# A fifth feature block in a seven-product (Strassen) matmul, and output stores by two column blocks

## The chip, the cores and the metric

The kernel runs on one core of one Trainium2 chip. The time is that of the device, in microseconds, for one execution of the whole program; less is better. TensorE (PE) does the matmuls, VectorE (DVE), ScalarE (ACT) and GpSimd (POOL) the elementwise work, and SyncE (SP) issues most DMAs; ACT issues some.

## What is computed

Decayed linear attention over 4 batches, 8 heads, 768 positions and 64 dimensions in blocks of 64, then a two-layer network with a leaky ReLU on 3072 tokens of 512 features (2048 hidden). All inputs are float32.

```python
for b in range(nb):                       # blocks of 64 positions
    intra = einsum('bhic,bhjc->bhij', qb, kb) * Dmask
    intra = einsum('bhij,bhjd->bhid', intra, vb)
    inter = einsum('bhid,bhde->bhie', qb * lam_pow, kv_state)
    out[:, :, sl] = intra + inter
    kv_state = lam_block * kv_state + einsum('bhsd,bhse->bhde', kb * rev_pow, vb)
x = out.transpose(0, 2, 1, 3).reshape(B * S, H * D)      # 3072 x 512
h = x @ w_in                                             # 3072 x 2048
return maximum(0.01 * h, h) @ w_out                      # 3072 x 512
```

## The kernel before

**Staging.** The 3072 tokens are 24 chunks of 128, or six groups of `T` = 512; two groups make a pair (`pr` = 0, 1, 2). The 2048 hidden features are eight blocks `p` of 256. A float32 operand is split into three parts, high, low and a middle one (`h`, `l`, `m`), and each product is three matmuls, one for each part.

First the attention of each chunk is done ("r"), and between the chunks the products with `w_in` ("up", group g, block p): 24 matmuls of 512 columns each. ACT applies the leaky ReLU and writes the tile `gs`, which goes to DRAM. For feature blocks below `NS` (4; `NS0` = 2 for the first pair) `sums` first makes six combinations on DVE, stored in `BB`; the others are stored plainly in `G`. The weights `w_out` are made ready meanwhile ("wo", "wp") and, for blocks below `NS`, `w_sums` ("ws") makes their combinations.

Then, from about 324 us, come the products with `w_out`, pair by pair. For a block under `NS`, the 2x2 block product (two groups against two halves of the features and of the outputs) is done with seven products, s(t, u), t = 1 to 7, instead of eight: unit u holds two feature blocks and 12 matmuls. Partial sums lie in the PSUM bank pairs X, Z, Y and V, with copies by ACT (`copy_banks`) and additions by ACT and DVE (`add_banks`) between the products. The other blocks are plain units n(p, group) of 24 matmuls. The last block's unit ("l") also transposes each of the four output column blocks on DVE (`turn_out`, L943) and stores them (`store_out`, L951); the very last group does this in `ending`.

**The ring.** Each unit loads its moving operand (L825, on SP), and ACT makes the high part (L828), DVE the low (L831) and the middle one (L835). There are five slots, so a unit's load is issued when the unit five places earlier has left PE. For product 4 a second block is loaded and subtracted first (L842, L843). PE's matmuls are at L723 (up) and L851 (units).

**Order.** `Plan` is a list scheduler: each operation is added with an engine, an assumed duration, the keys that it reads and writes, and a rank, mostly its place in the written list `seq`. `emit` takes whatever can start earliest by these durations, ties by rank, and so fixes the order on each engine ahead of time. A DMA is assumed to need 3.5 us more until it lands; a store on ACT counts 0.5 us and 0.1. Engines run their own order, so a wait holds up all that is queued behind it. `LEAD` lowers the rank of the preparation of units; `HOLD`, `WPR` and `WSR` shift the rank of steps in the last group's phase.

Of the kernel before, what the change touches and what calls it, by code (L numbers as in the profile page):

```python
# [166 lines left out]
def kernel(  # L167
# [35 lines left out]
    NS, NS0 = 4, 2  # L203
    WS0, WS1 = 1, 2
    LEAD = 8.0
    TURN_B = 2
    HOLD, WPR, WSR, LEAD0 = 0.15, 2.0, 0.0, 12.0
# [34 lines left out]
    gst = sb([P, 2, 2, T], "gs")  # L242
    gs = [gst[:, i] for i in range(2)]
# [3 lines left out]
    BB = [[dram.tile([P, 6 * 2 * T], F32, name=f"b{r}_{u}", tag=f"b{r}_{u}") for u in range((NS if r else NS0) // 2)] for r in range(NG // 2)]  # L247
# [405 lines left out]
    staging = [w32f, lowt.bitcast(F32), gs[1].rearrange("p f t -> p (f t)")]  # L653
    SK = [["w320", "w321"], ["low0", "low1"], ["gs1"]]
# [3 lines left out]
    def free_attention(x="att"):  # L658
        extra[x] = sb([P, NA if x == "att" else NB], x, F32R)

# [3 lines left out]
    def operand(z, p, t):  # L664

        if t >= 0:
            return W[p][z][:, t * NQ:(t + 1) * NQ]
        return more(z, p)[:, (-1 - t) * NQ:-t * NQ]
# [14 lines left out]

    def w_sums(p):

        j, jr, main, rest = (SK[0], SK[1], staging[0], staging[1]) if p >= NS0 else (["raw1", "zr"], ["raw2"], raw[1], raw[2])
        b = [main[:, i * NQ:(i + 1) * NQ] for i in range(4)] + [rest[:, i * NQ:(i + 1) * NQ] for i in range(3)]
        add("DMA", 1.5, lambda: nc.sync.dma_start(out=main, in_=WO[p]), [f"WO{p}0", f"WO{p}1"], j, rank=-3.0)

        def sub(o, x, y, op, reads, k_):  # L690
            add("DVE", 0.42, lambda: nc.vector.tensor_tensor(b[o], b[x], b[y], op=op), reads, k_)

        sub(5, 0, 1, ALU.subtract, j, jr)
        sub(1, 1, 3, ALU.add, [], j)
        sub(4, 1, 0, ALU.subtract, j, jr)
        sub(6, 2, 4, ALU.subtract, j, jr)
        for key, us, x, src, k_ in ((f"w{{}}{p}", 0.42, lambda z: W[p][z][:, NQ:2 * NQ], b[1], j),
                                   (f"e{{}}{p}", 0.95, lambda z: more(z, p), rest[:, :3 * NQ], jr)):
            h, l, m = [key.format(z) for z in "hlm"]
            add("ACT", 0.9 * us, lambda x=x, src=src: nc.scalar.activation(out=x(0), in_=src, func=AF.Copy, bias=0.0, scale=NEAR / S), k_, [h])  # L700
            add("DVE", us, lambda x=x, src=src: nc.vector.scalar_tensor_tensor(x(1), x(0).bitcast(F32), -S, src, op0=ALU.mult, op1=ALU.add),
                k_ + [h], [l])
            if p == NS - 1 and k_ is jr:
                add("ACT", 0.0, free_lows, [], jr + [m])
            minus(us, x, key)
# [71 lines left out]
    def sums(g, p, y, kg):  # L777
# [7 lines left out]
        d = BB[g // 2][p // 2].rearrange("p (k c g t) -> p k c g t", k=6, c=2, g=2)[:, :, p % 2, g % 2, :]  # L785
# [23 lines left out]
    def unit(src, keys, f=1, less=None):  # L809

        nonlocal n_ring
        j = slots[n_ring] if n_ring < len(slots) else RING[(n_ring - len(slots)) % NR]
        first, n_ring = j not in slots[:n_ring], n_ring + 1

        def wr(z):
            return [f"r{z}{j}"] + ([f"x{z}{j // 2}{cc}" for cc in range(GC)] if first and j < 4 else [])

        def m_slot():
            return ring[j][2].bitcast(F32)

        def g():
            return m_slot() if less is None else w32f

        def go():
            nc.sync.dma_start(out=m_slot().rearrange("p (f t) -> p f t", f=f), in_=src)  # L825

        def head():
            nc.scalar.activation(out=ring[j][0], in_=g(), func=AF.Copy, bias=0.0, scale=NEAR)  # L828

        def low():  # L830
            nc.vector.scalar_tensor_tensor(ring[j][1], g(), 1.0, ring[j][0].bitcast(F32), op0=ALU.mult, op1=ALU.subtract)  # L831

        def middle():
            h, l, m = ring[j]
            nc.vector.scalar_tensor_tensor(m, l.bitcast(F32), -S, h.bitcast(F32), op0=ALU.mult, op1=ALU.add)  # L835

        kg = [f"rm{j}"]
        add("DMA", 1.5, go, keys, wr("m"))
        if less is not None:
            x, k = less  # L840
            kg = ["w320", "w321"]
            add("DMA", 1.5, lambda: nc.sync.dma_start(out=w32f, in_=x), k, kg)  # L842
            add("DVE", 1.25, lambda: nc.vector.tensor_tensor(w32f, w32f, m_slot(), op=ALU.subtract), [f"rm{j}"], kg)  # L843
        add("ACT", 1.05, head, kg, wr("h"))
        add("DVE", 1.25, low, kg + [f"rh{j}"], wr("l"))
        add("DVE", 1.25, middle, [f"rh{j}", f"rl{j}"], [f"rm{j}"])
        return j
# [6 lines left out]
    def strassen(pr, t, u, lead):  # L854

        g = 2 * pr
        ps_ = (2 * u, 2 * u + 1)
# [3 lines left out]
        def block(kind):  # L861
            k = KINDS_B.index(kind)
            return BB[pr][u][:, k * 2 * T:(k + 1) * 2 * T], [f"{'B' if k < 4 else 'T'}{x}{p}" for x in (g, g + 1) for p in ps_]

        x, keys = block("6" if t == 4 else str(t))
        j = unit(x.rearrange("p (f t) -> p f t", f=1), keys, less=block("2") if t == 4 else None)
# [15 lines left out]
        add("PE", 0.227 * (13 if begins else 12), go, [f"r{z}{j}" for z in "hlm"] + [f"{'w' if w >= 0 else 'e'}{z}{p}" for z in "hlm" for p in ps_],  # L882
            ACC[d] + (ACC["Z"] if begins else []))

    def plain(pr, p, gi, lead, last=False, banks=None):
# [25 lines left out]
        for c in banks:  # L911
            some(c)
            turn_out(gi, c)
        for m in range(2):
            store_out(pr, gi, m, range(4), "AAAA")

    def ending(pr, gi, first, lead):
# [8 lines left out]
        for m in range(2):  # L926
            store_out(pr, gi, m, a, "SASA")
        for c in z:
            one(c)
        for m in range(2):  # L930
            for c in z:
                two(c, m * HT, HT)
                turn_out(gi, c, m * HT, HT)
            store_out(pr, gi, m, z, "SASA")

    otile = gst.rearrange("p x f (b c j) -> p (x f b) c j", c=4, j=C4)

    def turn_out(gi, c, lo=0, n=T):
        nonlocal n_o
        n_o += 1  # L940
        d, i = BANKS[gi][c]
        b, o = acc[d][i], otile[:, lo // C4:(lo + n) // C4, c, :]
        add("DVE", 0.1 + 0.6 * n / T, lambda: nc.vector.transpose(out=o, in_=b[:, lo:lo + n].rearrange("p (b i) -> p b i", i=C4)), [ACC[d][i]],  # L943
            [f"o{c}{m}" for m in range(lo // HT, (lo + n) // HT)] + (["gs0", "gs1"] if n_o <= 4 else []), rank=-1.5)

    def store_out(pr, gi, m, cs, queues):
        t0, n, w = (2 * pr + m) * T + gi * HT, HT // C4, len(cs) * C4

        def store(a, q):
            c0 = a * P + cs[0] * C4  # L950
            q.dma_start(out=out[t0:t0 + HT, c0:c0 + w].rearrange("(b i) j -> i b j", i=C4),  # L951
                        in_=otile[a * C4:(a + 1) * C4, m * n:(m + 1) * n, cs[0]:cs[-1] + 1, :].rearrange("i b c j -> i b (c j)"))

        for a, x in enumerate(queues):
            e, q = {"S": ("DMA", nc.sync), "A": ("ACT", nc.scalar)}[x]
            add(e, 0.5, lambda a=a, q=q: store(a, q), [f"o{c}{m}" for c in cs], [], rank=6.0 if len(cs) == 4 else -1.5)
# [5 lines left out]
    def add_banks(d, s):  # L962
        for i in range(2):
            y, key = w32[:, i, :], [f"w32{i}"]
            add("ACT", 0.6, lambda i=i, y=y: nc.scalar.copy(y, acc[s][i]), [ACC[s][i]], key, rank=-LEAD)
            add("DVE", 0.72, lambda i=i, y=y: nc.vector.tensor_tensor(acc[d][i], acc[d][i], y, op=ALU.add), key, [ACC[d][i]], rank=-LEAD)

    seq = [('a', 0), ('a', 1), ('a', 2), ('a', 3), ('wi', 5), ('b', 4), ('up', 0, 5), ('wi', 2), ('wi', 6), ('r', 4), ('r', 5), ('up', 0, 2), ('wi', 3), ('r', 6), ('up', 0, 6), ('r', 7), ('up', 0, 3), ('wi', 4), ('wi', 0), ('up', 0, 4), ('up', 1, 5, 0, 3), ('up', 1, 3), ('wi', 7), ('wi', 1), ('up', 1, 4), ('up', 0, 0), ('up', 1, 5, 3, 4), ('up', 1, 7), ('up', 0, 1), ('ls',), ('up', 1, 6), ('up', 0, 7), ('r', 8), ('up', 1, 0), ('lt',), ('r', 9), ('r', 10), ('r', 11), ('up', 1, 2), ('up', 1, 1)]
    nxt, n_out, begin = 3 * GC, 0, len(seq)
    ORDER = [4, 0, 3, 7, 2, 6, 5, 1]  # L970
# [18 lines left out]
    for pr in range(NG // 2):  # L989
# [7 lines left out]
        if pr:  # L997
            seq += [late[0], s(1, 0), late[1], s(1, 1), ("copy", "Z", "X"), late[2], s(6, 0), late[3], s(6, 1), ("copy", "Y", "Z"),
                    s(5, 0), s(5, 1), ("add", "Y", "V"), s(7, 0), s(7, 1), ("add", "V", "Z"),
                    s(3, 0), n(4, 0), s(2, 0), n(5, 0), s(3, 1), s(2, 1), n(6, 0), s(4, 0), s(4, 1), n(7, 0)]  # L1000
        else:
# [4 lines left out]
            put(("up", NG - 1, 2), ("ws", 0))  # L1006
            put(("up", NG - 1, 2), ("ws", 1))
            put(("up", NG - 1, 6), ("fr",))
            put(("up", NG - 1, 7), s(1, 0), ("copy", "Z", "X"))
            seq += [s(6, 0), ("copy", "Y", "Z"), s(5, 0), ("add", "Y", "V"), s(7, 0), ("add", "V", "Z"), s(3, 0), n(2, 0), s(2, 0), n(3, 1), s(4, 0), n(2, 1), ("ws", 2), n(3, 0), ("ws", 3)]  # L1010
            seq += [n(p, 0) for p in range(NS, NP)]
# [3 lines left out]
    for n, x in enumerate(seq):  # L1015
# [39 lines left out]
        elif x[0] == "add":  # L1055
            add_banks(*x[1:])
# [35 lines left out]
```

## Time and profile before

| | before |
|---|---|
| time, median of 3 (lowest to highest) | 598.83 us (598.8 to 599.8) |
| profiled execution: time / span | 598.83 us / 597.1 us |
| PE busy, matmuls | 586.2 us, 5336 |
| DVE / ACT / POOL busy | 406.7 / 299.2 / 134.0 us |
| DMA moved | 123.04 MB, mean 206 GB/s |
| granted TensorE clock | 1.000 |

The span is from the first to the last instruction of the program in the profile. Busy time is that in which an engine executes; issuing DMAs and waiting are not counted. Matmuls overlap in PE, so two neighbours start 0.23 us apart though each is listed with 0.39 us.

### The profile page before, as it was taken

The numbers are of one execution on the slowest core, as the hardware profiler recorded it, in microseconds if no ns is written. First come the engines' busy times: TensorE is split into PE (matmuls) and PEld (weight loads), VectorE is DVE, ScalarE is ACT, GpSimd is POOL, SyncE is SP. The second block draws the span as 40 slices with busy tenths as digits, with TensorE's granted clock in tenths as the row PEclk, the third lists the DMA queues.
The fourth block names the chain that finished last, engine by engine and source line by source line (L and its number), as shares of the span: only waits on it lengthen the run. The fifth ranks groups of instructions, "written<-read, shape, count | busy, mean of one in ns | idle before, by whom it ended". The sixth has DMA issues, their size and how long they took to land.

```text
span 597.1 us, 13281 instructions
## 1 busy us (share of the span) xinstructions
PE 586.2 (98%) x5336; PEld 485.0 (81%) x5336; DVE 406.7 (68%) x559; ACT 299.2 (50%) x468; POOL 134.0 (22%) x170
## 2 busy tenths in 40 slices
PE   7899999999999999999999999999999999999997
PEld 6778888888888888888788888888888888888886
DVE  4999883357365565465389889965689695788652
ACT  3788884345555565565598874331344223252300
POOL 2654770835636348121000000000000000000000
PEclk9999999999999999999999999999999999999999
DMA  8999855975899999886788865526467547394533
GB/s 205 238 292 242 245 171 132 247 195 132 240 284 260 239 269 232 247 259 224 244 273 273 298 196 206 162 89 190 128 198 223 175 144 193 121 259 164 177 107 70
DMA packets 163949, 123.04 MB, mean 206 GB/s; under 512 B 100400, under 2 KB 140592, under 8 KB 163888
## 3 DMA queue, kind: packets, MB, share of 16 engines
q1 hardware_dynamic: 148128, 112.75, 64.4%
q10 hardware_dynamic: 13200, 5.77, 3.8%
q0 software_dynamic: 2560, 3.68, 2.5%
q8 instruction: 42, 0.69, 0.5%
q14 instruction: 19, 0.16, 0.1%
HBM read 81.27 MB, written 40.89 MB: 205 GB/s over the span
## 4 chain that ended last, share of the span: by engine, by line
PE 91%; DVE 5%; DMA 2%; ACT 0%; issue 0%; SPq 0%; DVEq 0%
PE b L723 43%; PE po L851 13%; PE b L851 12%; PE psc L851 11%; PE pt L851 4%; PE po L335 4%; PE psc L335 3%; DMA xm<-g 1%; DVE wl L628 1%; DVE w L617 1%; DMA attb<-in_q_dram 1%; DVE w L616 1%; PE pt L425 1%; DVE att L474 0%; DVE xl L530 0%
## 5 line engine op out<-in xcount | busy, mean ns | idle before, releaser
L723 PE MATMUL b<-xh,wh 128*128 128x512 f32 (+2 forms) x392 | 103.6, 387 | 0.8 <-ACT xh L529 0.8
L723 PE MATMUL b<-xm,wm 128*128 128x512 f32 (+2 forms) x392 | 103.7, 393 | 0.0
L723 PE MATMUL b<-xl,wl 128*128 128x512 f32 (+2 forms) x392 | 103.5, 386 | 0.1
L828 ACT ACTIVATE xh<-xm 128x1024 fp32r<-128x1024 f32 x46 | 48.8, 1060 | 86.6 <-DMA xm<-g 40.9
L723 PEld LDWEIGHTS b<-xh,wh 128*128 128x128 f32 x392 | 72.7, 188 | 16.1 <-ACT xh L529 0.9
L723 PEld LDWEIGHTS b<-xl,wl 128*128 128x128 f32 x392 | 72.8, 188 | 15.2 <-DVE wl L628 0.5
L723 PEld LDWEIGHTS b<-xm,wm 128*128 128x128 f32 x392 | 71.2, 188 | 15.1 <-ACT b L742 0.4
L742 ACT ACTIVATE b<-b 128x512 f32<-128x512 f32 (+2 forms) x97 | 56.1, 581 | 54.5 <-PE b L723 54.4
L747 ACT ACTIVATE gs<-b 128x512 f32<-128x512 f32 (+2 forms) x97 | 56.8, 591 | 39.7 <-PE b L723 34.6
L831 DVE SCALAR_TENSOR_TENSOR xl<-xm,xh 128x1024 fp32r<-128x1024 f32 x46 | 56.0, 1218 | 26.4 <-ACT xh L828 25.5
L835 DVE SCALAR_TENSOR_TENSOR xm<-xl,xh 128x1024 fp32r<-128x1024 f32 x50 | 61.2, 1224 | 3.5
L484 POOL TENSOR_TENSOR att<-att 128x256 f32<-128x256 f32 x40 | 34.9, 873 | 37.9 <-DVE att L481 37.9
L616 DVE TENSOR_SCALAR w<-w 128x512 int32<-128x512 int32 x32 | 22.6, 706 | 27.2 <-ACT w L610 27.1
L396 POOL DMA_DIRECT2D attb<-in_q_dram x64 | 39.5, 624 | 2.9 <-issue 1.4
L445 POOL TENSOR_TENSOR att<-att 128x512 f32<-128x512 f32 (+1 forms) x20 | 24.9, 1244 | 63.4 <-PE po L335 47.4
L441 POOL TENSOR_TENSOR attb<-attb,att 128x512 f32<-128x512 f32 (+1 forms) x23 | 26.1, 1136 | 34.6 <-PE po L425 10.5
L851 PE MATMUL psc<-xm,wm 128*128 128x512 f32 x84 | 32.8, 391 | 0.1
L851 PE MATMUL psc<-xh,wh 128*128 128x512 f32 x84 | 32.7, 389 | 0.0
L851 PE MATMUL psc<-xl,wl 128*128 128x512 f32 x84 | 32.7, 389 | 0.0
L474 DVE TENSOR_TENSOR att<-psc,att 128x512 f32<-128x512 f32 x24 | 16.5, 688 | 21.9 <-PE psc L335 21.8
L617 DVE CUSTOM_DVE_ANT_0 w<-w,lows 128x1024 uint16<-128x1024 uint16 x32 | 26.2, 818 | 7.1 <-ACT lows L614 6.2
L828 ACT ACTIVATE raws<-raws 128x1024 fp32r<-128x1024 f32 x12 | 12.7, 1061 | 27.6 <-DMA raws<-g 18.1
(184 smaller groups left out, 1096.3 us busy)
## 6 DMA issues: line engine op xcount, KB each, us to landing
xm<-b SPq DMA_DIRECT2D x28, 512.0 KB, 3.8
g<-gs SPq DMA_DIRECT2D x27, 512.0 KB, 4.6
xm<-g SPq DMA_DIRECT2D x22, 512.0 KB, 4.2
b<-gs SPq DMA_DIRECT2D x20, 512.0 KB, 3.9
raws<-in_moe_w_in_dram SPq DMA_DIRECT2D x16, 512.0 KB, 5.2
raws<-in_moe_w_out_dram SPq DMA_DIRECT2D x16, 512.0 KB, 4.9
attb<-in_k_dram SPq DMA_DIRECT2D x48, 128.0 KB, 4.7
attb<-in_v_dram SPq DMA_DIRECT2D x24, 256.0 KB, 4.7
```

What stands on the lines that cost most here:

```text
L335: nc.tensor.matmul(dst[HALF[cols]], lhsT=lhsT[HALF[rows]], rhs=rhs[HALF[rows]], start=start, stop=True, skip_group_check=True)
L396: (move if nm == "k" else carry)(0.55 if nm == "k" else QSL, lambda o=o, z=z, e=nc.sync if nm == "k" else nc.gpsimd: e.dma_start(out=o.rea ...
L484: add("POOL", 0.7, lambda new=new, j=j: nc.gpsimd.tensor_tensor(state[(j + 1) % 4], new, _bc(lam_c, 2, D), op=ALU.mult), [f"st{j % 4}", "f ...
L616: add("DVE", 0.42, lambda: nc.vector.tensor_scalar(d, d, 3, None, op0=ALU.logical_shift_left), [], [key])
L617: add("DVE", 1.0, lambda: nc.vector.tensor_tensor(d, d, low, op=ALU.add), [kl], [key])
L723: nc.tensor.matmul(dst, lhsT=w[z][:, kk * 2 * P + f * P:kk * 2 * P + (f + 1) * P], rhs=x[z][:, kk, toks], start=start and kk == 0, stop=kk ...
L742: add("ACT", ns, lambda b=b: nc.scalar.activation(out=b, in_=b, func=AF.Copy, bias=0.0, scale=S + 1.0), [], [kb], rank=-1.5)
L747: add("ACT", t, lambda o=o, x=s_: nc.scalar.activation(out=o, in_=x, func=AF.Prelu, bias=0.0, scale=(1.0 + 1.0 / S) / (WS * U), alpha=0.01 ...
L828: nc.scalar.activation(out=ring[j][0], in_=g(), func=AF.Copy, bias=0.0, scale=NEAR)
L831: nc.vector.scalar_tensor_tensor(ring[j][1], g(), 1.0, ring[j][0].bitcast(F32), op0=ALU.mult, op1=ALU.subtract)
L835: nc.vector.scalar_tensor_tensor(m, l.bitcast(F32), -S, h.bitcast(F32), op0=ALU.mult, op1=ALU.add)
L851: nc.tensor.matmul(dst, lhsT=lhs(z), rhs=ring[j][z][:, col:col + n], start=first and z == 0, stop=z == 2, skip_group_check=True)
```

## The change

`NS` goes from 4 to 5: in the second and third pair of groups block 4 joins the seven-product scheme as a unit of its own, with one feature block, 6 matmuls and loads of half the size. Its weight sums need room: `sums_five` takes it from the tiles `w32`, `gs0`, `gs1` and the end of `attb`. Output tile and staging change with it: the output tile holds two column blocks (`gs0`; in `ending` a second one in `gs1`), so a group's output leaves in two halves, each of eight stores with rows of 256 bytes, and the third column block is transposed into the place of the first. In the later pairs `add_banks` and product 4 use `gs0` for what they kept in `w32`. The work list `seq` after its thirteenth entry, the order of the up products, the order of the units in each pair and four planner constants are written anew.

```diff
-    NS, NS0 = 4, 2
+    NS, NS0 = 5, 2
-    LEAD = 8.0
+    LEAD = 10.0
-    HOLD, WPR, WSR, LEAD0 = 0.15, 2.0, 0.0, 12.0
+    HOLD, WPR, WSR, LEAD0 = 0.45, 2.0, 4.0, 12.0
...
+    BY = [[min(2, n - p) for p in range(0, n, 2)] for n in (NS0, NS)]
...
+    def sums_five(src, h, l, m):
+        n = 2 * NQ
+        cut = [slice(0, n), slice(n, 3 * NQ)]
+        add("ACT", 0.0, lambda: free("w32"), [], ["w320", "w321", h, l])
+        add("ACT", 0.85, lambda: nc.scalar.activation(out=fifth(0)[0], in_=src, func=AF.Copy, bias=0.0, scale=NEAR / S), ["gs1"], [h])
+        for i in range(2):
+            add("DVE", (0.7, 0.42)[i], lambda i=i: nc.vector.scalar_tensor_tensor(
+                    fifth(1)[i], fifth(0)[0].bitcast(F32)[:, cut[i]], -S, src[:, cut[i]], op0=ALU.mult, op1=ALU.add), ["gs1", h], [l])
...
-    def unit(src, keys, f=1, less=None):
+    def unit(src, keys, f=1, less=None, n=2 * T):
...
-        ps_ = (2 * u, 2 * u + 1)
+        nb = BY[pr > 0][u]
+        ps_ = range(2 * u, 2 * u + nb)
...
-        add("PE", 0.227 * (13 if begins else 12), go, ...
+        add("PE", 0.227 * (6 * nb + begins), go, ...
...
-        for c in banks:
-            some(c)
-            turn_out(gi, c)
-        for m in range(2):
-            store_out(pr, gi, m, range(4), "AAAA")
+        for cs in (banks[:2], banks[2:]):
+            for c in cs:
+                some(c)
+                turn_out(gi, c)
+            for m in range(2):
+                store_out(pr, gi, m, cs, "AAAA", 0.0)
...
-            add(e, 0.5, lambda a=a, q=q: store(a, q), [f"o{c}{m}" for c in cs], [], rank=6.0 if len(cs) == 4 else -1.5)
+            add(e, 0.5, lambda a=a, q=q: store(a, q), [f"{to}{c % 2}{m}" for c in cs], [], rank=rank)
...
-    ORDER = [4, 0, 3, 7, 2, 6, 5, 1]
+    ORDER = [2, 0, 4, 3, 1, 7, 5, 6]
...
         if pr:
-            seq += [late[0], s(1, 0), late[1], s(1, 1), ("copy", "Z", "X"), late[2], s(6, 0), late[3], s(6, 1), ("copy", "Y", "Z"),
-                    s(5, 0), s(5, 1), ("add", "Y", "V"), s(7, 0), s(7, 1), ("add", "V", "Z"),
-                    s(3, 0), n(4, 0), s(2, 0), n(5, 0), s(3, 1), s(2, 1), n(6, 0), s(4, 0), s(4, 1), n(7, 0)]
+            seq += [[
+                late[0], s(1, 0), s(1, 2), s(1, 1), late[1], ("copy", "Z", "X"), late[2], s(5, 0), s(6, 0), s(6, 2), s(2, 0),
+                s(6, 1), s(5, 1), ("copy", "Y", "Z"), s(5, 2), s(7, 1), ("add", "Y", "V", pr), s(7, 0), s(7, 2), s(2, 2),
+                ("add", "V", "Z", pr), n(5, 0), s(2, 1), s(4, 1), s(3, 0), s(3, 1), n(6, 0), s(4, 0), s(4, 2), s(3, 2), n(7, 0)], [
+                late[1], s(1, 0), s(1, 1), s(1, 2), late[0], ("copy", "Z", "X"), late[2], s(6, 2), s(6, 0), s(6, 1), s(5, 0),
+                s(5, 2), ("copy", "Y", "Z"), s(3, 0), s(7, 1), s(5, 1), s(2, 1), s(7, 2), s(7, 0), ("add", "Y", "V", pr),
+                ("add", "V", "Z", pr), s(2, 2), n(6, 0), s(4, 1), s(3, 1), s(3, 2), s(2, 0), n(5, 0), s(4, 0), s(4, 2), n(7, 0)
+            ]][pr - 1]
...
```

In these lists late[i] is the plain unit of the pair before for its second group and block NS + i.

## The prediction

> **What bounds the kernel now.** I read the page first: the busy shares and the slices.
>
> ```profile
> span 597.1 us, 13281 instructions
> PE 586.2 (98%) x5336; PEld 485.0 (81%) x5336; DVE 406.7 (68%) x559; ACT 299.2 (50%) x468; POOL 134.0 (22%) x170
> PE   7899999999999999999999999999999999999997
> PEclk9999999999999999999999999999999999999999
> ```
>
> TensorE is busy for 98% at the full granted clock. Where the other 2% lies is asked of the windows, one for each stage (busy us and instruction counts, then clock, DMA share, GB/s):
>
> ```profile
> 0.00:60.00 60.00, 54.02 (x998) 43.45 (x1002) 50.38 (x84) 41.83 (x73) 28.04 (x31) 1.00 0.94 244
> 60.00:290.00 230.00, 230.00 (x2948) 192.07 (x2947) 129.23 (x233) 129.32 (x229) 106.00 (x140) 1.00 0.81 223
> 290.00:360.00 70.00, 69.59 (x365) 56.82 (x364) 56.38 (x75) 56.54 (x88) 0.00 (x0) 1.00 0.82 269
> 360.00:440.00 80.00, 80.00 (x354) 66.21 (x353) 61.13 (x64) 25.23 (x30) 0.00 (x0) 1.00 0.48 150
> 440.00:520.00 80.00, 80.00 (x354) 66.15 (x353) 60.79 (x58) 27.32 (x30) 0.00 (x0) 1.00 0.58 179
> 520.00:597.00 77.00, 72.63 (x331) 60.33 (x329) 48.76 (x49) 18.92 (x21) 0.00 (x0) 1.00 0.53 157
> ```
>
> PE idles 6.0 us before 60 us, 0.4 us from there to 520 us, and 4.4 us at the tail. So between 60 us and the tail the time is the number of matmuls times their spacing: a matmul taken out there is time taken out, and any new PE wait is time added. The chain that ended last gives the spacing, and the only feed of PE that it passes through after 300 us:
>
> ```profile
> 349.11 5.50 DMA xm<-g
> ...
> 356.99 1.24 DVE xm L835
> ...
> 401.67 2.72 PE psc L851 x12
> ```
>
> Twelve 512-column matmuls take 2.72 us, 0.227 us each.
>
> How near PE is to waiting is read from the timeline of one unit of the last pair of groups, the plain unit of block 4: its load is issued, its last part is written by DVE, its first matmul starts.
>
> ```profile
> 524.32 0.53 SPq L825 DMA_DIRECT2D xm<-g  x1
> ...
> 532.54 1.23 DVE L835 SCALAR_TENSOR_TENSOR xm<-xl,xh 128x1024 fp32r<-128x1024 f32 x1
> ...
> 535.06 0.39 PE L851 MATMUL psc<-xh,wh 128*128 128x512 f32 x1
> ```
>
> The load goes out when the unit five places earlier ends (the ring has five slots), so four units, 48 matmuls or 10.9 us, must cover it. It needs 533.77 - 524.32 = 9.45 us; its third matmul, the first to read that part, starts at 535.51, so it has 1.7 us to spare. The same unit one pair earlier (issue 442.56, last part 450.19 + 1.23) needed 8.9 us; the quickest, away from crowds (issue 420.74, last part done 428.37), 7.6 us.
>
> **The change part by part.** *Matmuls.* A plain feature block costs two groups x 24 = 48 matmuls for a pair of groups. Half a seven-product unit has 6, and 7 x 6 = 42. Two pairs of groups take up block 4, so 12 matmuls go: 12 x 0.227 = **-2.72 us**, on the path, since 60 to 592 us is PE without a gap. All other products stay in number. The Trainium skill ("TensorE: Matmul & The Clock Gate", section "Wait — 56ns, not 53.3ns?") gives 215.7 ns from start to start for 512 columns on a warm clock; by it the sum would be -2.59 us, and the 227 ns of this trace decides.
>
> *Feeding the ring.* A half unit takes one of the five slots but covers only 1.36 us. In the new order of the second pair, the unit plain(5, group 0) has the two whole units of s7, then the halves of s7 and s2, right ahead of it: 12 + 12 + 6 + 6 = 36 matmuls, 8.2 us where the least was 10.9. In the third pair plain(6, group 0) has the same 36. Several units before these have 42, 9.5 us. With the 0.45 us before the third matmul, 36 gives 8.6 us and 42 gives 10.0 us. Against the three needs read above: 7.6 leaves no wait, 8.9 costs 0.3, 9.45 costs 0.85. So the wait is 0 to 0.85 us per pair, and I take 0.3: the 9.45 is partly a load that landed in 5.4 us where the median is 4.2, amid deferred output stores, and these now get rank 0 for 6 and leave before the crowded stretch. Two pairs: **+0.6 us** (0 to 1.7).
>
> *DVE and ACT.* A full unit costs DVE 1.22 + 1.22 (L831, L835) and ACT 1.06 (L828). Half units I put between the 0.42 us of 128x256 and the 1.22 of 128x1024, at 0.65 (L966, 128x512, took 0.69). A pair goes from 22 full units and two subtractions (56.1 us) to 20 full, 7 halves and three subtractions (48.8 + 9.1 + 3.1 = 61.0): +4.9 us of DVE in 79 us of which 61 were busy. The weight sums of block 4 are one more set: four L691 at 0.43, narrow L701 and L636 at 0.42, wide ones near 0.96, slightly more in two pieces: 4.7 us of DVE and 2.5 of ACT, placed between the plain units near 400 us, needed only after some 45 us of PE work. The sums of block 4 in groups 2 to 5 add three L783 of 0.43 each: 5.2 us in four places. None is on the path while DVE has 13.6 us free in 290 to 360 us and 18.9 in 360 to 440 us. If that cover went, each microsecond that DVE is late is one of PE.
>
> *DMA.* Per pair seven half loads and one second operand (256 KB each) stand for two plain loads (512 KB): +1 MB and six more SP issues of 0.3 to 0.5 us; block 4's sums write 768 KB instead of 512 KB in each of four groups. About 3 MB on 123 MB, at shares of 0.48 to 0.58: nothing on the path, except where it slows a landing, which the bounds above hold.
>
> *Output stores.* Five group outputs now leave in two halves: 80 stores of 64 KB by ACT for 40 of 128 KB. What one set costs the queue behind it is in the timeline of ACT, and what a store takes in the DMA view:
>
> ```profile
> 408.50 4.98 ACTq L951 DMA_DIRECT2D out_dram<-gs  x8
> 413.52 1.06 ACT L828 ACTIVATE xh<-xm 128x1024 fp32r<-128x1024 f32 x1 [7.00 <-DMA out_dram<-gs]
> ```
>
> ```profile
> out_dram<-gs ACTq DMA_DIRECT2D x40, 128.0 KB, 3.5
> out_dram<-gs ACTq DMA_DIRECT2D x8, 64.0 KB, 2.2
> ```
>
> Both halves use the same two columns of the output tile, so a new wait comes in: the third transpose waits on DVE until the first half's eight stores have landed. First transposes done at 405.7, eight issues of 0.45 to 0.62 us, 2.2 us to land: 411.5 to 412.9. The planner counts 0.5 us for an ACT store and no landing, so it lets the transposes go 1.6 to 3 us too early, and the lows of the next units queue behind them on DVE, as heads do behind the stores on ACT. The unit prepared there in the trace (L835 at 409.60, done 410.83) is used at 420.71: 9.9 us to spare. After the other group's output it was 8.7 us (428.37 to 437.04). I cost it at nothing; bound 0 to 1.5 us in all, were a half unit the next to be used.
>
> The 512-byte output rows become 256-byte rows. The Trainium skill ("DMA: Bandwidth & Descriptors", Specifications) asks for at least 512 B for line rate and says that smaller ones are read, modified and written. The rows above speak mildly of it: 2 x 2.2 us against 3.5, a quarter dearer, not twice.
>
> *Order.* The first twelve entries of the work list (as far as the fourth weight block) stay, so I leave the 6.0 us of the start as they are. Later ones are permuted, which cannot gain more than the 0.4 us of idle PE there; it can lose. The tail keeps its form: no change.
>
> Sum: -2.72 + 0.6 = -2.1 us. The profiled execution took 598.83 us (span 597.1, 1.7 around it), and that is also the median of the runs shown: 598.83 - 2.1 = **596.7 us**, span 595.0.
>
> **The rivals.** *Slower: the ring runs dry in the seven-product stretch.* If loads, DVE and ACT need x us from issue to last part, a pair loses x - 8.6 at the 36-matmul window, and about one and a half ring turns lose x - 10.0 each. The 2.72 us are gone at 1.36 per pair, x = 10.0. With one more 1.2 us DVE operation queued ahead of the crowded unit (9.45 + 1.2 = 10.65), a pair loses 2.05 + 1.0, two pairs 6.1: 602.2 us. For it: DVE is busy 90% and more there (527 to 538 us), and adds its bank additions. Against: both trace values lie below 10.0, and half units ask for less. Chance 0.14.
>
> *The new order of the front costs what the products save.* From 290 to 360 us DVE and ACT are busy 81% and DMA 82%; the chain passed through a just-in-time unit at 349 to 358 us (0.3 us lost). Missing it by one load (4.2 us), half covered by another ready unit, costs 2.1: 598.8 us. One such miss gives no change; two, 600.9. Chance 0.20.
>
> *Store rows dear.* If 256-byte rows doubled the engines' time, loads beside them would land in 5.4 and not 3.8 us in both pairs: +1.6 x 2, 599.9 us. The landing rows speak against. The rule quoted above from the Trainium skill's "DMA: Bandwidth & Descriptors" (Specifications) would make it so. Chance 0.04.
>
> *Nothing is lost anywhere*, and the start wins the 0.4 us of 40 to 60 us: 595.7 us. Chance 0.12.
>
> **How the numbers follow.** My forecast has the remaining 0.50. Some 0.2% (1.2 us, below 597.6 or above 600.0) is what a measurement of this kernel can tell from none. Faster: forecast and last rival, 0.62. The front's miss gives 0.11 same and 0.09 slower; the store rows 0.04 same; the dry ring 0.01 same and 0.13 slower: same 0.16, slower 0.22. The range runs from 595.6 to 600.8: it holds the forecast with its unknown waits (596.1 to 599.3) and single misses; about 0.17 lies above it. Without the slower cases I would give 595.7 to 597.9.
>
> **What would show it.** Right: PE instructions 12 fewer; 360 to 580 us with PE busy throughout; a span near 595. Step by step: the plain units named above start within 0.5 us of the unit before; L831 of the units after an output sits behind L943, which waits for out_dram, with no PE gap; 64 KB stores land near 2.2 us. Wrong: PE idle above 1 us in any 20 us window after 60 us, with "DVE xm" or "ACT xh" as the releaser in the seven-product stretch (the dry ring), or a gap before 360 us (the order).

## The result, and the profile after

The changed kernel takes 630.76 us (median of four runs, 629.04 to 633.11) where the kernel before, beside it, takes 599.32: ratio 1.0536, 95% interval 1.0511 to 1.0560. It is slower by 31 us; the forecast was 596.7 us, and its range ended at 600.8. The profiled execution took 629.04 us, span 627.3 us.

The page of the changed kernel, busy shares and the rows of PE and its clock:

```profile
span 627.3 us, 13473 instructions
PE 592.6 (94%) x5324; PEld 484.1 (77%) x5324; DVE 426.1 (68%) x605; ACT 303.4 (48%) x480; POOL 134.9 (22%) x170
...
PE   7899999999999999999999999998879999789993
...
PEclk9999999999999999999999999998979999979997
```

The twelve matmuls are gone (5336 to 5324). PE is nevertheless listed busy for 6.4 us longer, and two dips stand in a row that was all nines. The windows say where (columns as in the prediction), first two of before, then three of after:

```profile
420.00:470.00 50.00, 50.00 (x222) 41.30 (x221) 39.13 (x37) 18.79 (x22) 0.00 (x0) 1.00 0.58 178
...
520.00:560.00 40.00, 40.00 (x177) 33.05 (x176) 30.45 (x29) 14.66 (x17) 0.00 (x0) 1.00 0.67 210
```

```profile
420.00:470.00 50.00, 40.77 (x157) 31.33 (x156) 29.52 (x32) 15.03 (x20) 0.00 (x0) 0.90 0.52 142
...
520.00:560.00 40.00, 33.46 (x132) 25.25 (x131) 25.87 (x27) 11.14 (x14) 0.00 (x0) 0.91 0.60 162
...
616.00:627.00 11.00, 0.44 (x4) 0.24 (x2) 1.85 (x4) 0.00 (x0) 0.00 (x0) 0.69 0.50 103
```

Here the count of matmuls is a better ruler than busy time, because a matmul on a slowed clock counts as busy for longer. Of 222 matmuls in the first window 157 are left, of 177 in the second 132. Missing are 65 and 45, at 0.227 us 14.8 and 10.2 us. The last matmul ends at 616.44 us, 10.8 us before the end of the span, against 4.4 us before the change: 6.4 more. PE's idle time up to 360 us goes from 6.4 to 8.0 us. Sum: -2.7 + 14.8 + 10.2 + 6.4 + 1.6 = 30.3, and the spans differ by 30.2 us.

Both dips follow the output of a pair's groups. The chain that ended last runs through the first dip, and through the tail, like this (start, us, what):

```profile
423.34 5.12 DMA xm<-b
...
428.48 0.32 ACTq L984
...
436.16 2.56 PE pt L874 x6
...
446.31 4.96 DMA xm<-b
451.29 4.45 DMA out_dram<-gs
456.02 1.31 DVE gs L976 x2
457.33 1.12 DVE xl L866
458.47 1.24 DVE xm L868
...
617.58 1.51 DMA out_dram<-gs
619.09 0.71 DVE gs L976
```

Read the piece at 446 to 460 us from below. PE waits for the low and the middle part of a unit (L866 and L868, L831 and L835 before). DVE writes them late because two transposes of the output (L976, L943 before) stand ahead of them. These wait for a store of the first half to land, and that store was issued only at 451.29 us, when a unit's *load*, issued by SP at 446.31, had landed. A store has no use for that load's data. The two have the same completion semaphore, number 103: by the trace's events, the DMAs that SP and ACT issue share eight of them (100 to 103, 105 to 108), and an issue waits until the DMA that had its semaphore before has landed. The load in its turn had waited for a slot of the ring, which PE had to free. So there is a loop: PE frees a slot, the load goes out and lands, a store goes out and lands, DVE transposes and splits, PE goes on. The chain goes through such a hand-over twice in this dip; the first time a store waits until 428.46 us for the load issued at 423.34 us (both semaphore 102), and the heads on ACT stand behind it.

How long ACT is held is in its timeline (issues in a row, then the next operation with its idle time and releaser):

```profile
423.47 6.87 ACTq L984 DMA_DIRECT2D out_dram<-gs  x8
430.44 0.85 ACT L710 ACTIVATE gs<-gs 128x768 fp32r<-128x768 f32 x1 [9.77 <-DMA out_dram<-gs]
...
442.85 8.76 ACTq L984 DMA_DIRECT2D out_dram<-gs  x7
451.66 1.06 ACT L865 ACTIVATE xh<-xm 128x1024 fp32r<-128x1024 f32 x1 [7.77 <-DMA out_dram<-gs]
```

Before, the longest row of issues ahead of the tail was the 4.98 us that the prediction shows; here eight take 6.87 and seven 8.76 us, and ACT can make no high part (L865, L828 before) meanwhile. From its first issue to its last, a set was already long before the change: two of the five were spread over 8.3 and 9.0 us (from 441.10 and 522.86 us), with operations of ACT between the issues. The ten sets of the changed kernel last 3.9 to 10.0 us so measured. What is new is that there are twice as many, and that ACT stands still in the long ones. The waits behind output stores (total us, times, longest), first of before, then of after:

```profile
ACT xh L828 <- DMA out_dram<-gs: 9.4, 2, 7.0
ACT raws L828 <- DMA out_dram<-gs: 4.9, 1, 4.9
```

```profile
DVE gs L976 <- DMA out_dram<-gs: 24.2, 6, 9.6
ACT xh L865 <- DMA out_dram<-gs: 19.7, 3, 8.3
ACT raws L865 <- DMA out_dram<-gs: 13.8, 3, 6.6
ACT gs L710 <- DMA out_dram<-gs: 9.8, 1, 9.8
```

ACT's go from 14.3 to 43.3 us, DVE's from nothing to 24.2. PE's own longest waits after 360 us are these:

```profile
PE po L874 <- DVE xl L866: 5.2, 1, 5.2
PE b L874 <- ACT b L993: 4.5, 1, 4.5
```

These two stops make up 9.7 of the 15.8 us that PE is idle in the two windows; the rest are shorter ones. The first is that of the chain above. The second, at 549.9 us, is for a bank copy (L993, L960 before) that began right behind the transposes, and the chain comes to it in the same way: a load from 539.77 to 544.62 us, a store issued at 544.65, the transposes at 548.49.

### The profile page after: what moved, and what is told of

It is laid out like the page before. It is cut to its first block, busy times and chain, and to the rows that moved or that the text cites. A ratio compares the mean times of both kernels' runs of the same rounds, so it can differ in the third digit from the quotient of the medians.

```text
span 627.3 us, 13473 instructions
## 1 busy us (share of the span) xinstructions
PE 592.6 (94%) x5324; PEld 484.1 (77%) x5324; DVE 426.1 (68%) x605; ACT 303.4 (48%) x480; POOL 134.9 (22%) x170
## 4 chain that ended last, share of the span: by engine, by line
PE 83%; DMA 8%; DVE 4%; SPq 1%; ACT 1%; issue 1%; ACTq 0%; DVEq 0%
PE b L756 40%; PE po L874 13%; PE b L874 10%; PE psc L874 10%; PE po L335 3%; PE pt L874 3%; PE psc L335 3%; DMA xm<-b 2%; DMA out_dram<-gs 2%; DMA b<-raws 1%; DMA raws<-in_moe_w_in_dram 1%; DMA attb<-in_k_dram 1%; DVE xm L868 1%; DMA attb<-in_v_dram 1%; SPq L360 1%; DVE xl L866 1%
## 5 line engine op out<-in xcount | busy, mean ns | idle before, releaser
L865 ACT ACTIVATE xh<-xm 128x1024 fp32r<-128x1024 f32 (+1 forms) x53 | 51.2, 970 | 86.0 <-DMA xm<-b 23.4
L775 ACT ACTIVATE b<-b 128x512 f32<-128x512 f32 (+2 forms) x97 | 56.5, 583 | 60.4 <-PE b L756 60.2
L756 PEld LDWEIGHTS b<-xl,wl 128*128 128x128 f32 x392 | 72.8, 188 | 14.8
L866 DVE SCALAR_TENSOR_TENSOR xl<-xm,xh 128x1024 fp32r<-128x1024 f32 (+1 forms) x53 | 58.7, 1108 | 24.1 <-ACT xh L865 23.7
L780 ACT ACTIVATE gs<-b 128x512 f32<-128x512 f32 (+2 forms) x97 | 56.7, 592 | 34.6 <-PE b L756 31.4
L868 DVE SCALAR_TENSOR_TENSOR xm<-xl,xh 128x1024 fp32r<-128x1024 f32 (+1 forms) x58 | 64.1, 1106 | 5.2 <-DVE xl L866 0.5
L616 DVE TENSOR_SCALAR w<-w 128x512 int32<-128x512 int32 x32 | 18.4, 574 | 19.9 <-ACT w L610 19.9
L874 PE MATMUL psc<-xh,wh 128*128 128x512 f32 x78 | 30.3, 389 | 0.0
L874 PE MATMUL psc<-xl,wl 128*128 128x512 f32 x78 | 30.3, 389 | 0.0
L874 PE MATMUL psc<-xm,wm 128*128 128x512 f32 x78 | 30.3, 389 | 0.0
L612 ACT ACTIVATE lows<-raws 128x512 uint16<-128x512 uint32 x32 | 25.2, 786 | 1.7 <-DMA raws<-in_moe_w_in_dram 0.8
```

What stands on the lines that cost most here:

```text
L756: nc.tensor.matmul(dst, lhsT=w[z][:, kk * 2 * P + f * P:kk * 2 * P + (f + 1) * P], rhs=x[z][:, kk, toks], start=start and kk == 0, stop=kk ...
L775: add("ACT", ns, lambda b=b: nc.scalar.activation(out=b, in_=b, func=AF.Copy, bias=0.0, scale=S + 1.0), [], [kb], rank=-1.5)
L780: add("ACT", t, lambda o=o, x=s_: nc.scalar.activation(out=o, in_=x, func=AF.Prelu, bias=0.0, scale=(1.0 + 1.0 / S) / (WS * U), alpha=0.01 ...
L865: add("ACT", 0.15 + 0.9 * k, lambda: nc.scalar.activation(out=at(h), in_=g(), func=AF.Copy, bias=0.0, scale=NEAR), kg, wr("h"))
L866: add("DVE", 0.15 + 1.1 * k, lambda: nc.vector.scalar_tensor_tensor(at(l), g(), 1.0, at(h).bitcast(F32), op0=ALU.mult, op1=ALU.subtract), ...
L868: add("DVE", 0.15 + 1.1 * k, lambda: nc.vector.scalar_tensor_tensor(at(m), at(l).bitcast(F32), -S, at(h).bitcast(F32), op0=ALU.mult, op1=A ...
```

## The experiments

Ratios are to the kernel before on the same chip, with the 95% interval. "Lost" is missing matmuls in a window times 0.227 us. Each run has one profile.

### Which part of the change costs it

**e1** takes the kernel before (`NS` = 4, its order and constants) and lets outputs leave by two column blocks, their stores with rank 0.0 for 6.0 and the second output tile in `ending`, as in the change:

```diff
-    gst = sb([P, 2, 2, T], "gs")
-    gs = [gst[:, i] for i in range(2)]
+    gs = [sb([P, 2, T], f"gs{i}") for i in range(2)]
...
-        for c in banks:
-            some(c)
-            turn_out(gi, c)
-        for m in range(2):
-            store_out(pr, gi, m, range(4), "AAAA")
+        for cs in (banks[:2], banks[2:]):
+            for c in cs:
+                some(c)
+                turn_out(gi, c)
+            for m in range(2):
+                store_out(pr, gi, m, cs, "AAAA", 0.0)
```

> The kernel before with the output part of the change alone: a two-column output tile and two sets of eight stores per group, no fifth block, the old order. Hand-over theory (the second half's transposes wait at the head of VectorE's queue until the first half's stores have landed, and the units' low and middle parts stand behind them): most of the 31 us is here, 615 to 630 us, with TensorE idle after each output and a tail several us longer than 4.4 us. Ring theory (the half-size units leave the ring of five slots dry): nothing is here, 598 to 600 us. If the order of the work list is to blame: also 598 to 600 us.

Measured 619.16 us, 1.0319 (1.0281 to 1.0356): +20 us, 9.1 lost in 420 to 470 us and 8.6 in 520 to 560 us. The tail is 4.4 us, as in the kernel before.

**e2** takes the changed kernel with the output tile of four column blocks, eight stores of 128 KB to a group. To make room it leaves out the middle part of block 4's wide weight sums (three operations of some 3 us in all on DVE and ACT) and reads the high part in its place.

```diff
-    gs = [sb([P, 2, T], f"gs{i}") for i in range(2)]
+    gst = sb([P, 2, 2, T], "gs")
+    gs = [gst[:, i] for i in range(2)]
...
-                store_out(pr, gi, m, cs, "AAAA", 0.0)
...
+            store_out(pr, gi, m, range(4), "AAAA")
```

> The changed kernel with the output tile of four column blocks and the eight 128 KB stores of before, so the fifth block and the new order alone. To make room, the middle part of block 4's wide sums is not made (its high part is read in its place), which leaves out three one-time operations of some 3 us on VectorE and ScalarE; all matmuls, loads and units stay. Hand-over theory: the predicted gain shows, 596 to 598 us. Ring theory: 615 us or more, with TensorE idle inside the seven-product stretch. Order theory (the permuted front loses time): 600 us or more with the idle time before 360 us.

Measured 613.85 us, 1.0227 (1.0194 to 1.0260): +14.5 us, 7.0 and 3.0 lost in the two windows, and 3.1 us of idle PE between 60 and 290 us. No transpose waits for a landing here, yet two sets of eight issues hold ACT for 9.3 and 8.5 us in a row (from 419.54 and 444.00 us). So each part stalls by itself, and in the first window the halves aren't needed for it. Together they cost about what they cost singly (20 + 14.5 against 31).

### What about the stores costs it

The first theory was the one that the prediction had named and priced too low: DVE's transposes wait for landings, and lows queue behind them. The rival was that the stores hold up ACT.

**e3** tells the planner that a store of an output takes 3 us more to land, so that DVE does other work first:

```diff
+            plan.slack = 3.0
             add(e, 0.5, lambda a=a, q=q: store(a, q), [f"{to}{c % 2}{m}" for c in cs], [], rank=rank)
+            plan.slack = 0.0
```

> The changed kernel, but the planner counts 3 us until an output store on ScalarE has landed; nothing else, only the order on the engines changes. Hand-over theory, in the form that the transposes are merely queued too early: 600 to 610 us, the transposes move behind the lows of the next units and wait little at the head of VectorE's queue. If the chain of stores itself is too long (each store waiting for a free completion semaphore that a load holds), the order helps little: 620 us or more. Ring theory: no change, 629 to 632 us.

Measured 629.50 us, 1.0494 (1.0453 to 1.0534). The waits of e3:

```profile
ACT xh L865 <- DMA out_dram<-gs: 26.6, 4, 10.9
ACT raws L865 <- DMA out_dram<-gs: 8.3, 2, 5.8
DVE gs L976 <- DMA out_dram<-gs: 3.1, 1, 3.1
```

DVE's wait fell from 24.2 to 3.1 us and the time stayed. The first theory falls, in the form that the transposes are merely queued too early: when DVE isn't made to wait, the heads on ACT wait as they did (34.9 us for 33.5).

**e4** issues two of each four stores from SP, **e5** all four from GpSimd (the last group's stay on SP and ACT in turn, as they were):

```diff
-                store_out(pr, gi, m, cs, "AAAA", 0.0)
+                store_out(pr, gi, m, cs, "SASA", 0.0)     # e4
+                store_out(pr, gi, m, cs, "PPPP", 0.0)     # e5: 0.65 us and 3 us to land, to the planner
```

> The changed kernel with the eight stores of each half issued in turn by SyncE and ScalarE, as the last group does already. If the time of eight issues on one queue (8 x 0.5 us) makes the hand-over long: each hop is 2 us shorter, and the planner counts the landing of the stores on SyncE, so 605 to 620 us. If the wait for landing and semaphores rules: 622 to 632 us, or worse, since loads now stand behind waiting stores on SyncE. Ring theory: no change, 629 to 632 us.

> The changed kernel with the stores of each half issued by GpSimd, which is idle after 290 us and has completion semaphores of its own; the planner counts 3 us for their landing. Queue theory (ScalarE stands still at the stores, each waiting for transposes or for a completion semaphore that a unit's load holds, and the high parts of the next units stand behind it): 596 to 603 us, no TensorE gap over 1 us after the outputs; what is left is the hand-over of the two-column tile, in the tail above all. Hand-over theory (VectorE's wait for the landing is what costs): 610 us or more, as the transposes wait just the same. Ring theory: 615 us or more.

Measured 607.14 us, 1.0122 (1.0089 to 1.0155), and 608.38 us, 1.0159 (1.0135 to 1.0182). 22 to 24 of the 31 us are gone either way. The windows of e4 where the dips were:

```profile
420.00:470.00 50.00, 49.81 (x220) 40.78 (x219) 39.61 (x42) 21.07 (x26) 0.00 (x0) 1.00 0.73 209
...
520.00:560.00 40.00, 37.56 (x165) 30.64 (x164) 31.60 (x34) 15.73 (x20) 0.00 (x0) 1.00 0.69 203
```

220 matmuls for 157, and 165 for 132, with the same stores, rows and tile to hand over. The planner orders the engines a little differently in both, since it counts the landing of a store on SP or GpSimd; e3 gave it such a count for stores on ACT and gained nothing. The heads on ACT still wait 19.8 us behind stores in e4, but at most 5.6 us at a time, where the changed kernel has 8.3 and, with L710, 9.8. **The Trainium skill** ("Trainium Kernel Development and Optimization", section "Key Constraints") says that DMAs from several queues run on the same 16 engines and that issuing from several only saves issue time. The runs agree, if issue time is taken to hold what the issuing engine waits for: that was worth 22 to 24 us here.

**e6** is e2 with its stores on GpSimd, **e8** the kernel before with its stores there (the same edit of the queue letters).

> The fifth block alone as in the earlier run (output tile of four column blocks; the middle part of block 4's wide sums left out), with its stores issued by GpSimd. Queue theory: the fifth block costs nothing by itself and brings its 12 matmuls, 595 to 598 us. Ring theory: the gaps of the earlier run stay, 608 us or more. Order theory: a remainder before 380 us of 1 to 4 us, 598 to 601 us.

> The kernel before with only the queue of its output stores changed, to GpSimd. TensorE waits for nothing there, so queue theory, hand-over theory and ring theory all expect 597 to 600 us; it says whether the queue is worth anything by itself, and is the kernel that the changed one with the same stores is to be held against.

e6: 605.66 us, 1.0100 (1.0085 to 1.0116); e8: 599.68 us, 1.0006 (0.9994 to 1.0017). The stores on ACT cost the kernel before nothing; 8 of e2's 14.5 us come from them, 6.1 in the first window (218 matmuls in e6 for 191). In the second, e6 has 165 for e2's 164, as e4 has 165 with half its stores on ACT: what e2 lost there is most likely something else, the order of the third pair (e10, below). So the stores on ACT bite only in company with the fifth block and its order or, to judge by e1, with the halves; e1 with its stores elsewhere wasn't run.

**e7** leaves the stores on ACT and has GpSimd issue the units' loads, so that SP's loads no longer share semaphores with the stores:

```diff
-        add("DMA", 1.5 * k, lambda: nc.sync.dma_start(out=at(m).bitcast(F32).rearrange("p (f t) -> p f t", f=f), in_=src), keys, wr("m"))
+        add("DMA", 1.5 * k, lambda: nc.gpsimd.dma_start(out=at(m).bitcast(F32).rearrange("p (f t) -> p f t", f=f), in_=src), keys, wr("m"))
...
-            add("DMA", 1.5 * k, lambda: nc.sync.dma_start(out=g(), in_=less[0]), less[1], kg)
+            add("DMA", 1.5 * k, lambda: nc.gpsimd.dma_start(out=g(), in_=less[0]), less[1], kg)
```

> The changed kernel with the stores left on ScalarE, but the loads of the units issued by GpSimd, so that no store waits for a semaphore that a load holds. If that waiting is what makes a set of eight stores last 9 to 20 us: sets of 4 to 5 us again, and 603 to 612 us (the eight issues and the landing stay, and the tail). If ScalarE simply stands behind transposes that wait for landings: 620 us or more. Loads that are slower from this queue would show as later landings, 5 us and more, in either case.

Measured 618.54 us, 1.0322 (1.0263 to 1.0380): 12 us back. Windows of e7:

```profile
420.00:470.00 50.00, 46.51 (x190) 37.36 (x189) 34.11 (x38) 16.54 (x21) 8.32 (x15) 0.93 0.61 172
...
520.00:560.00 40.00, 38.16 (x159) 30.56 (x158) 31.77 (x35) 14.93 (x20) 7.15 (x13) 0.96 0.68 193
```

Lost are 7.3 and 4.1 us for 14.8 and 10.2, and a set lasts 3.8 to 5.8 us from first issue to last. The loads land little later than from SP (medians of the DMA view 4.2 and 4.5 us for 3.8 and 4.1). So the loads that hold semaphores make up about half of the dips. The other half, argued from the timelines and not isolated: heads stand behind stores which themselves wait for transposes, and behind eight issues of about half a microsecond.

### The tail

**e9** is e4 with the second half of the last pair's outputs in the second output tile, so that these transposes have no landing to await. **e10** is e9 with the third pair's units in the second pair's order.

```diff
+            to = "z" if pr == NG // 2 - 1 and cs == banks[2:] else "o"     # e9, handed to turn_out and store_out
...
-            ]][pr - 1]
+            ]][0]                                                         # e10
```

> The changed kernel with the stores on two queues, and in the last pair the second half of the plain output goes to the second output tile, so that no transpose of the last group waits for stores that have just been issued. If the hand-over of the two-column tile makes the tail (7.1 us from the last matmul to the end of the span against 4.4 before): the tail is 4.4 to 5 us, and 604 to 605.5 us against 607.1. If the tail is just the time of the stores: no change, 606 to 608 us.

> As the one with the mended tail, and the third pair takes the unit order of the second pair. If the third pair's own order makes its 2.8 us of idle TensorE (0.6 us in the second pair): 2 to 2.5 us less, 601.5 to 603.5 us. If what is lost there comes from anything else: no change.

e9: 605.87 us, 1.0120 (1.0076 to 1.0164), not to be told from e4's by the ratios; its tail is 5.7 us where e4's is 7.1. e10: 601.77 us, 1.0055 (1.0036 to 1.0074), tail 4.4 us as in the kernel before, and 172 matmuls in 520 to 560 us where e4 has 165 and e9 161. The third pair's own order cost some 4 us, 1.3 of them in the tail.

What e10 still has over the kernel before is little enough to be listed. The ring waits as the prediction had it; PE at plain(5, 0):

```profile
463.54 0.39 PE L874 MATMUL psc<-xl,wl 128*128 128x512 f32 x1
464.06 0.50 PE L874 MATMUL psc<-xm,wm 128*128 128x512 f32 x1
```

0.52 us from start to start for 0.23: 0.3 us lost, at the first matmul that reads the middle part. In the third pair 0.86 us are lost at this place, between the matmuls at 544.54 and 545.63 us. And there is the front:

```profile
230.00:290.00 60.00, 58.52 (x713) 47.87 (x712) 33.57 (x65) 32.59 (x59) 15.75 (x20) 1.00 0.81 244
290.00:360.00 70.00, 69.12 (x359) 55.24 (x358) 54.09 (x71) 55.32 (x87) 0.00 (x0) 1.00 0.74 245
```

1.5 and 0.9 us idle, and 0.8 more between 60 and 230 us, where the kernel before had none, 0.4 and none.

### The front, and the planner's constants

**e11** is e10 with `seq` of the front and `ORDER` as before, **e12** the same with stores on GpSimd, **e15** is e11 with the last group's up products in the order 0, 1, 5, 2, 3, 6, 4, 7 (block 4's sums two places later):

```diff
-    ORDER = [2, 0, 4, 3, 1, 7, 5, 6]
+    ORDER = [4, 0, 3, 7, 2, 6, 5, 1]          # e11, and seq up to the first pair as before
...
-                for p in (ORDER if g < NG - 1 else range(NP))]
+                for p in (ORDER if g < NG - 1 else (0, 1, 5, 2, 3, 6, 4, 7))]     # e15
```

> As the one with one order for both pairs, and the work list and the order of the up products before the last group put back to what they were, with the fifth block kept. Order theory for the remainder (3 us of idle TensorE between 240 and 380 us against 1.3 before): 597.5 to 600 us. If block 4's sums cost this by themselves, in whatever order: 601 to 603 us.

> The same three mends with the stores on GpSimd and not on SyncE and ScalarE in turn. If the two-queue run still loses by heads behind stores (19.8 us of such waits on ScalarE, though few reach TensorE): 0.5 to 2 us less than on two queues, 596 to 599 us. If GpSimd's stores delay loads (one load took 8.3 us beside them): equal or up to 2 us slower.

> The kernel with the old front, with the last group's up products in the order 0, 1, 5, 2, 3, 6, 4, 7, so that no more than two blocks with sums stand in a row. If the row of five holds the gs buffers: the 2.9 us of idle TensorE at 320 to 350 us fall under 1 us, 598.5 to 599.5 us against 601.2. If ScalarE's load in that stage is the cause: no change, 600.5 to 602 us; if weights for the first units come too late in this order: slower.

e11: 601.18 us, 1.0045 (1.0031 to 1.0060). e12: 600.99 us, 1.0029 (1.0010 to 1.0048). e15: 602.45 us, 1.0058 (1.0043 to 1.0073). The same windows in e11:

```profile
230.00:290.00 60.00, 60.00 (x723) 49.71 (x722) 31.56 (x60) 35.11 (x62) 16.29 (x21) 1.00 0.79 239
290.00:360.00 70.00, 67.86 (x354) 54.30 (x353) 55.88 (x75) 55.11 (x86) 0.00 (x0) 1.00 0.78 261
```

The old order cures 230 to 290 us and loses 2.1 us in 290 to 360 us instead. e15 has 74 matmuls between 340 and 360 us where e11 has 89; PE waits there for the parts of the first units, and not for an up product. In e1, without block 4, the two windows lose 0 and 0.3 us. But so they do in the changed kernel itself, with block 4:

```profile
230.00:290.00 60.00, 59.96 (x721) 49.38 (x720) 34.61 (x67) 33.96 (x60) 16.70 (x21) 1.00 0.83 250
290.00:360.00 70.00, 69.72 (x365) 56.30 (x364) 55.70 (x73) 55.06 (x87) 0.00 (x0) 1.00 0.76 252
```

Up to 356 us the changed kernel, e4, e5, e9 and e10 run the same operations in the same order on every engine (but for two neighbouring matmuls at 44 us), and yet PE is idle for 1.3, 2.8, 4.6, 2.7 and 3.2 us between 60 and 360 us. So a good part of this is a spread between executions. In the fourteen profiles with block 4 it is 1.3 to 4.6 us, in the four of these with the old order 1.9 to 3.0, and in the three without block 4 (before, e1, e8) 0.4 to 1.3: block 4 in the front seems to cost some 2 us, whatever the order, and one profile can't give it more closely. PE's longest waits there are for ACT's two operations on an up product (L775, L780) in e10 and e11; whether ACT's order or the buffers of `gs` are behind it stays open.

**e13** and **e14** give e10 and e11 the constants of before: `LEAD` 8, `HOLD` 0.15, `WSR` 0.

> The kernel with two-queue stores, mended tail and one order for both pairs, with the constants of before (LEAD 8, HOLD 0.15, WSR 0). If the constants make the idle TensorE of 2.4 us at 240 us and 1.5 us at 320 to 350 us: 598 to 600 us against 601.8. If the fifth block's sums make it: 601 to 603 us.

> The same with the old front as well, so that only the fifth block, the unit orders, the output tile and the two-queue stores differ from before. If constants and front together make the rest: 597 to 599 us, under the kernel before. If block 4's sums in the last group cost it: 600 to 602 us, with 2 to 3 us of idle TensorE at 320 to 340 us.

611.16 us, 1.0203 (1.0171 to 1.0235), and 611.75 us, 1.0219 (1.0202 to 1.0236). In e13 PE's longest waits after 360 us are for the middle parts (L868): 4 us in small waits, at most 0.8 us each. This is what the rival of the dry ring looked like: the units' parts come out late again and again, and PE loses about 3 us in each of three stretches (360 to 380, 440 to 470 and 520 to 560 us). With the change's constants it doesn't happen. The three constants were put back together, so that `LEAD` is to blame isn't shown.

No version with block 4 beat the kernel before; e12 comes nearest, and its interval lies above 1.

## Why the prediction was wrong

**The step that failed is "Output stores": "I cost it at nothing; bound 0 to 1.5 us in all".** Taking half of the stores off ACT, or all, gave back 22 to 24 us; in e4 it was 21.8 of the dips' 25.0 and 3.7 of the tail. Three things in it were wrong. It took a set of stores as eight issues of a fixed length, 0.45 to 0.62 us; a set lasts as long as what its issues wait for, transposes and semaphores, and held ACT for as much as 8.76 us in a row. (The trace of before had sets spread over 8.3 and 9.0 us; the prediction read the one of 4.98.) It took the slack of 8.7 to 9.9 us from units as the old order prepared them, and compared one delay with it; in the chain shown, ACT's and DVE's delays come one after the other. That the units after an output are tighter in the new lists is likely, since the half units cover less, but wasn't measured. And it worked out the wait on DVE, where it was easy to see, and gave ACT's queue half a sentence: the before kernel's own waits had 14.3 us of heads behind stores in them, hidden only as long as nothing was added. e3 shows that the wait it worked out isn't the one that counts.

**"The tail keeps its form: no change"** was wrong by 6.4 us. The last group's third and fourth transposes go into the tile whose stores are under way (2.9 us at 619.09 us), a wait that the step on the stores had seen for the other groups and that the tail's step left out. The tile alone doesn't make it, as e1 has the same tile and a tail of 4.4 us. By the profiles 3.7 us go with the stores on two queues (e4), 1.4 with the second tile (e9) and 1.3 with the third pair's list (e10).

**"DVE and ACT … None is on the path while DVE has 13.6 us free"** was wrong by some 2 us in the front, as far as the spread lets one say; in the changed kernel's own profile it was 0.9 us between 60 and 360 us. Free time averaged over 70 us doesn't say whether the operations between two up products can be had in time. The rival on the front's order had the size (2.1 us for one miss) but not the cause: the loss is there in the old order too (e11, 2.1 us).

**The rivals** ended at 595.7 to 602.2 us, so none of them is what happened; the mechanism was named only in the step that set it at nothing. The sign given for the dry ring, PE idle with a high or middle part as the releaser, was met in part (1.8 and 3.0 us of PE's waits after 360 us), but the loads were not late: xm<-b took 3.8 us to land before and after. Parts of a unit can be late by the load or by the queue of the engine that makes them, and this sign doesn't tell which.

**What held.** The matmuls, to the instruction: 12 fewer, at 0.227 us. The ring: 0.3 us per pair was taken, bounds 0 to 0.85; e10 has 0.30 and 0.86. The dry ring stayed away, as expected with a chance of 0.14 against it, and e13 shows that this hangs on the constants. Rows of 256 bytes aren't the cause of the dips: e4 and e5 have the same rows without them. The price read for these rows, "2 x 2.2 us against 3.5, a quarter dearer", was no price, though: it set eight stores of the quiet end against forty, most of which left in a crowd. The eight stores of 128 KB from 572.90 us, in quiet too, took 2.0 to 2.5 us to land, no longer than the 64 KB ones (1.9 to 2.7). That the rows didn't matter to the dips was luck, as far as that reading goes. Order of units was priced only for the front; the third pair's list cost 4 us more than the second's (e10), which no step had.

With the stores, the tail and the third list mended, the balance of e10 is -2.7 for matmuls against 2.8 us in the front up to 360 us, 1.2 in the ring and 0.7 in smaller waits: +2.0 by the spans (599.1 against 597.1 us). The matmuls saved are worth what was forecast for them; in e10 the front gives as much back.

## What to carry to other kernels

A DMA issue on a computing engine isn't only half a microsecond of work but a place in a queue: ask for each what it waits for (its data, and the landing of whatever had its semaphore before), and what compute stands behind it. Where a resource is handed over within a set of transfers, follow the hand-over round until it comes back to the engine that bounds the kernel; if it does, a delay can feed itself and the slack of one unit is no bound. In the waits view, read the waits that are hidden today, for they are what the next change will bring out.

## What the runs showed of the hardware

Idle gaps of PE cost more than their length. After the gaps of the changed kernel the granted clock fell to 0.91, 0.91, 0.92 and 0.83 in stretches of 20 us (420 to 480 and 540 to 560 us), and matmuls took twice as long: six in 2.56 us, 0.427 us each, in the line at 436.16 us of the chain shown. The 21 matmuls on a slowed clock, in three stretches from 435.67, 459.76 and 552.30 us, took 9.1 us where 21 x 0.227 is 4.8: some 4 of the 25 us in the two dips. The Trainium skill ("TensorE: Matmul & The Clock Gate", section "Part 1: The HAM clock gate") says that an idle window of about 3.4 us sets the clock to half, 426.7 ns for 512 columns (section "Wait — 56ns, not 53.3ns?"); the 427 ns agree with it. As to the window, the gaps of 5.2 and 4.5 us come ahead of two of the slow stretches; ahead of the first, from 435.67 us, the trace has only three gaps of about 0.8 us in a row, with a matmul after each.

What an issuing engine waits for stops all that it does. The Trainium skill ("DMA: Bandwidth & Descriptors", section "Anatomy of one DMA — SWDGE (gpsimd) path") says that a wait for a semaphore takes place on the issuing sequencer before dispatch. The trace agrees, for issues from ACT: 8.76 us from the first of seven issues to the end of the last, and 7.77 us without an operation on ACT, in the timeline above.
